# Decoding float64 weights with one 32-bit integer add on GpSimd in place of a masked two-term sum

## The chip, the cores and the metric

The kernel runs on one core of a Trainium2 chip. The metric is the device time of one execution in microseconds (us). Five engines work side by side: TensorE (PE in the profile, its weight loads PEld), VectorE (DVE), ScalarE (ACT), GpSimd (POOL) and SyncE (SP), which issues all DMAs of this kernel.

## The reference

Three layers over 2304 tokens: attention that keeps the 32 largest scores of each row, a first MLP with `g = h * cos(h)`, and a mixture of eight experts whose gate is normalised eight times over rows and columns.

```python
scores = scale * np.matmul(q, k.transpose(0, 1, 3, 2))      # (4, 8, 576, 576)
kth = np.partition(scores, -32, axis=-1)[..., -32:-31]
scores = np.where(scores >= kth, scores, -1e9)
...
h = x @ w_in;  g = h * np.cos(h);  x = g @ w_out            # w_in 512x2048, w_out 2048x512
...
for e in range(8):
    out += P[:, e:e + 1] * (np.maximum(x @ w1[e], 0.0) @ w2[e])
```

The weights `w_in` and `w_out` come as float64. The chip's engines compute in float32, so the kernel turns each float64 number, two 32-bit words, into one float32 first.

## The kernel before

The first MLP's weights are decoded in 32 blocks of 128x512 numbers, 16 of `w_in` and 16 of `w_out`. For each block `decode` loads both words of every number (`d_raw`, 512 KB), and then makes nine compute instructions: three on ScalarE that read the words (lines 349 and 351) or finish the sign (350), one Abs on ScalarE (352), two on VectorE (348 shifts and flips a bit of the high word into `d_mag`; 354 masks the sign and the exponent out), and three on GpSimd (353 multiplies the magnitude by the sign, 355 multiplies the low word's part by the signed power of two, 356 adds the two). The result lies in `win_s` or `wout_s` in SBUF and is also written to DRAM (`win_d`, `wout_d`) for later use. `d_raw` and `d_mag` are rings of four buffers; the sign takes one of the five `raw` buffers.

The program starts with three tiles of 128 tokens ("first attention" and "first mlp"): 3 tiles x 8 heads = 24 attention tiles, each with a chain of top-32 steps on VectorE (lines 480, 483, 484), softmax on ScalarE (486, 487) and GpSimd (485, 489, 491), transposes and products on TensorE (472, 496, 553). Between them stand the decode blocks. When tile 0 has its attention and all of `win_s`, its first product (650), gate (613 to 620), transposes (660) and second product (672) follow; that needs all of `wout_s`. Only when the three tiles are through the first MLP (`x2fh` and `x2fl` complete) can TensorE begin the expert products of these tokens ("fill", lines 396 to 398), which have no other input but weights and fill every gap of TensorE from then on while the attention of the other tokens runs on VectorE.

The order is not written by hand. `Plan` takes every operation with an estimated cost, its readers and writers, and a priority by engine and class (`PRIORITY`), and walks a list schedule: each engine takes the ready operation of the best priority. The costs in the `put` calls are the planner's own. In the class "decode" come the blocks; on VectorE their priority stands between the first MLP and the first attention, on GpSimd behind both. Where TensorE would stand idle in the opening, the plan inserts small matmuls that compute nothing needed (line 1088, on `ident` and `ones`).

Of the kernel before, what the change touches and what calls it, by code (L numbers as in the profile page):

```python
# [12 lines left out]
I32 = mybir.dt.int32  # L13
U32 = mybir.dt.uint32
AF = mybir.ActivationFunctionType
ALU = mybir.AluOpType
# [6 lines left out]
HALF_PI = 1.5707963267948966  # L23
# [48 lines left out]
class Plan:  # L72
# [15 lines left out]
    def buf(self, pool, shape, dtype, name):  # L88
        return Buf(self, pool, shape, dtype, name)
# [18 lines left out]
    def add(self, eng, cost, emit, reads=(), writes=(), prio=0.0, func=None, nbytes=0):  # L108
        op = Op()
        op.eng, op.cost, op.emit, op.func, op.bytes = eng, cost, emit, func, nbytes  # L110
        k = len(self.ops)
        op.prio = (prio, k)
        deps = set()

        def norm(acc):
            for a in acc:
                if isinstance(a, tuple) and isinstance(a[0], View):
                    b, lo, _ = a[0].span
                    yield b, lo + a[1], lo + a[2]
                elif isinstance(a, View):  # L120
                    yield a.span
                elif isinstance(a, Buf):
                    yield a, 0, 1 << 30
                else:
                    yield a

        pools = set()
        for b, lo, hi in norm(reads):
            pools.add(b.pool)
            for l, h, i, wr in b.log:  # L130
                if wr and l < hi and lo < h:
                    deps.add(i)
        for b, lo, hi in norm(writes):
            pools.add(b.pool)
            for l, h, i, wr in b.log:
                if l < hi and lo < h:
                    deps.add(i)
        for b, lo, hi in norm(writes):
            b.log = [e for e in b.log if not (lo <= e[0] and e[1] <= hi)]
            b.log.append((lo, hi, k, True))  # L140
        for b, lo, hi in norm(reads):
            b.log.append((lo, hi, k, False))
        for p in pools:
            for old in self.pools[p].get("after", ()):
                deps.update(self.users.get(old, ()))
                self.users[p + "<"] = True
        for p in pools:
            self.users.setdefault(p, []).append(k)
        deps.discard(k)
        op.deps = deps  # L150
        self.ops.append(op)
        return k
# [95 lines left out]
def fused_kernel(tc, kq, vv, w_in, w_out, w_gate, w1, w2, out, B=4):  # L248
# [4 lines left out]
    V, A_, G_, T_ = nc.vector, nc.scalar, nc.gpsimd, nc.tensor  # L253
# [27 lines left out]
    def put(eng, cost, emit, reads=(), writes=(), func=None, nbytes=0):  # L281
        return add(eng, cost, emit, reads, writes, PRIORITY[eng][CLASSES.index(work)], func, nbytes)

    def dma(dst, src, nbytes, reads=(), writes=(), slow=False):
        put("SP", 650.0 if slow else 475.0, lambda: nc.sync.dma_start(dst(), src()), reads, writes, nbytes=nbytes)
# [5 lines left out]
    cols = buf("cst", [128, 4], F32, "cols")  # L291
# [3 lines left out]
    put("POOL", 500, lambda: make_identity(nc, ident.ap), writes=[ident])  # L295
    put("DVE", 70, lambda: V.memset(ones.ap, 1.0), writes=[ones])
    put("DVE", 70, lambda: V.memset(zero.ap, 0.0), writes=[zero])
    for i, c in enumerate((HALF_PI, 768.0, -768.0)):
        put("DVE", 60, lambda i=i, c=c: V.memset(cols.ap[:, i : i + 1], c), writes=[(cols, i, i + 1)])
    x_d = buf("dram", [128, 4, NT], F32, "x_d")  # L300
    lg_d = buf("dram", [16, NT], F32, "lg_d")
# [35 lines left out]
    def decode(src, keep, part, low):  # L337

        raw, mag, sgn = d_raw(), d_mag(), raw_r()
        lb, lv = low
        dma(lambda: raw.ap, lambda: src.bitcast(I32), 1 << 19, writes=[raw])
        hi = lambda dt: raw.ap.bitcast(dt).rearrange("p (n t) -> p n t", t=2)[:, :, 1]
        lo = lambda: raw.ap.bitcast(U32).rearrange("p (n t) -> p n t", t=2)[:, :, 0]
        magf = lambda: mag.ap.bitcast(F32)
        put("DVE", 335, lambda: V.tensor_scalar(mag.ap, hi(I32), 3, 0x40000000, op0=ALU.logical_shift_left, op1=ALU.bitwise_xor), [raw], [mag])
        put("ACT", 613, lambda: A_.activation(sgn.ap, hi(F32), AF.Identity, bias=cols.ap[:, 1:2]), [raw, cols], [sgn])
        put("ACT", 613, lambda: A_.activation(sgn.ap, sgn.ap, AF.Sign, bias=cols.ap[:, 2:3]), [sgn, cols], [sgn])  # L350
        put("ACT", 520, lambda: A_.activation(lv(), lo(), AF.Copy, scale=2.0**-52), [raw], [lb])
        put("ACT", 520, lambda: A_.activation(magf(), magf(), AF.Abs), [mag], [mag])
        put("POOL", 1225, lambda: G_.tensor_tensor(magf(), magf(), sgn.ap, op=ALU.mult), [mag, sgn], [mag])
        put("DVE", 335, lambda: V.tensor_scalar(sgn.ap.bitcast(I32), mag.ap, -8388608, None, op0=ALU.bitwise_and), [mag], [sgn])
        put("POOL", 1225, lambda: G_.tensor_tensor(lv(), lv(), sgn.ap, op=ALU.mult), [lb, sgn], [lb])
        put("POOL", 1225, lambda: G_.tensor_tensor(lv(), magf(), lv(), op=ALU.add), [mag, lb], [lb])
        dma(keep, lv, 1 << 18, [lb], [part])

    def fresh(src, keep, part, low):
        if wide:  # L360
            decode(src, keep, part, low)
        else:
            dma(low[1], lambda: src, 1 << 18, writes=[low[0]])
            dma(keep, low[1], 1 << 18, [low[0]], [part])
# [762 lines left out]
```

## Time and profile before

| what | value |
|---|---|
| time, median of 3 runs (lowest to highest) | 2396.32 us (2395.92 to 2397.65) |
| profiled execution's own time | 2397.71 us |
| its span | 2395.9 us |
| TensorE busy | 2337.6 us (98%) |
| VectorE busy | 1844.4 us (77%) |
| ScalarE busy | 1368.1 us (57%) |
| GpSimd busy | 1287.4 us (54%) |

The page also cuts the span into 40 slices of 60 us and gives each engine's busy share in tenths. In the trace, a stretch of the span can be asked for busy time by engine, for groups of instructions by line and tile with their mean duration, and for what ended an engine's idle time.

### The profile page before, as it was taken

How to read it: one execution, taken by the hardware profiler on the slowest of the kernel's cores; microseconds unless marked ns; L12 is line 12 of the kernel's file. 1: busy time of each engine (PE TensorE's matmuls, PEld its weight loads, DVE VectorE, ACT ScalarE, POOL GpSimd, SP SyncE). 2: the span in 40 equal slices, each digit the busy share in tenths (PEclk: the TensorE clock that was granted, in tenths of full speed). 3: DMA queues.
4: the chain of work that ended last, by engine and by line, in shares of the span. 5: the costliest groups of instructions: out<-in, count | busy, mean ns of one | idle time of the engine just before them, and what ended most of it. 6: DMA issues, size and time to landing. Idle time of an engine off the chain costs nothing.

```text
span 2395.9 us, 34290 instructions
## 1 busy us (share of the span) xinstructions
PE 2337.6 (98%) x11439; PEld 1931.1 (81%) x11439; DVE 1844.4 (77%) x3371; ACT 1368.1 (57%) x2752; POOL 1287.4 (54%) x1352
## 2 busy tenths in 40 slices
PE   7889899999989999999999999999999999999999
PEld 5545699989867888888888898888888888888887
DVE  6986999999989999995166887876666666666665
ACT  7887888888878777775366776222322232222221
POOL 6986687888887666664411046433333344444440
PEclk9999999999999999999999999999999999999999
DMA  7642355554532344333343333122222221111101
GB/s 216 199 127 93 110 162 149 165 177 143 160 91 85 99 122 124 122 93 111 115 140 107 103 115 91 49 75 75 75 75 75 79 67 41 39 36 36 36 23 49
DMA packets 152465, 242.29 MB, mean 101 GB/s; under 512 B 14624, under 2 KB 61808, under 8 KB 152288
## 3 DMA queue, kind: packets, MB, share of 16 engines
q1 hardware_dynamic: 152288, 240.10, 33.4%
q8 instruction: 90, 1.47, 0.3%
q14 instruction: 87, 0.71, 0.1%
HBM read 208.18 MB, written 31.87 MB: 100 GB/s over the span
## 4 chain that ended last, share of the span: by engine, by line
PE 78%; DVE 9%; POOL 6%; ACT 3%; issue 2%; DMA 1%; SPq 0%; POOLq 0%; ACTq 0%; DVEq 0%
PE y L396 11%; PE y L398 11%; PE y L397 11%; PE g L398 3%; PE g L396 3%; PE g L397 3%; PE t L496 3%; PE h L398 2%; PE h L396 2%; PE h L397 2%; DVE wk L483 2%; DVE m L484 2%; PE t L522 1%; PE y L411 1%; PE y L408 1%
## 5 line engine op out<-in xcount | busy, mean ns | idle before, releaser
L371 POOL TENSOR_TENSOR wlo<-raw,whi 128x512 fp32r<-128x512 f32 x336 | 447.9, 1337 | 145.0 <-ACT whi L369 110.9
L484 DVE MAX8 m<-wk 128x8 f32<-128x576 f32 x432 | 318.4, 749 | 3.6
L971 DVE SCALAR_TENSOR_TENSOR acc<-y,P,acc 128x512 f32<-128x512 f32 x308 | 228.5, 747 | 98.0 <-PE y L398 97.4
L369 ACT ACTIVATE whi<-raw 128x512 fp32r<-128x512 f32 x416 | 258.5, 627 | 70.1 <-PE y L398 26.9
L483 DVE MATCH_REPLACE8 wk<-m,wk 128x576 f32<-128x576 f32 x288 | 213.9, 743 | 1.4
L396 PE MATMUL y<-whi,gh 128*128 128x512 f32 x448 | 181.7, 406 | 0.0
L398 PE MATMUL y<-whi,gl 128*128 128x512 f32 x448 | 176.2, 393 | 0.0
L396 PE MATMUL y<-gh,xh 128*128 128x512 f32 x450 | 176.0, 391 | 0.2
L397 PE MATMUL y<-wlo,gh 128*128 128x512 f32 x448 | 175.6, 392 | 0.0
L398 PE MATMUL y<-gh,xl 128*128 128x512 f32 x450 | 175.1, 389 | 0.0
L397 PE MATMUL y<-gl,xh 128*128 128x512 f32 x450 | 175.1, 389 | 0.0
L496 PE MATMUL t<-ident,ex 128*128 128x128 f32 (+1 forms) x720 | 129.0, 277 | 25.5 <-POOL ex L491 14.3
L496 PEld LDWEIGHTS t<-ident,ex 128*128 128x128 f32 (+1 forms) x720 | 84.4, 135 | 69.4 <-POOL ex L491 19.3
L478 ACT ACTIVATE sc<-s 128x288 f32<-128x288 f32 x288 | 116.6, 405 | 28.4 <-PE s L469 17.0
L486 ACT ACTIVATE ex<-sc,m 128x576 f32<-128x576 f32 x144 | 111.1, 771 | 33.0 <-DVE m L484 32.6
L491 POOL TENSOR_SCALAR ex<-ex,m 128x576 f32<-128x576 f32 x144 | 110.2, 765 | 36.2 <-DVE m L490 28.8
L514 ACT ACTIVATE ath<-t 64x128 fp32r<-64x128 f32 (+3 forms) x272 | 104.3, 395 | 32.1 <-PE t L496 31.3
L480 DVE MAX8 m<-sc 128x8 f32<-128x576 f32 x144 | 107.4, 746 | 18.6 <-ACT sc L478 18.5
L487 ACT ACTIVATE ex<-ex,m 128x576 f32<-128x576 f32 x144 | 111.3, 773 | 6.2 <-POOL m L485 1.9
L483 DVE MATCH_REPLACE8 wk<-m,sc 128x576 f32<-128x576 f32 x144 | 106.8, 742 | 0.3
L396 PEld LDWEIGHTS y<-gh,xh 128*128 128x128 f32 x450 | 84.5, 188 | 19.0 <-DVE acc L967 0.7
L398 PEld LDWEIGHTS y<-whi,gl 128*128 128x128 f32 x448 | 84.1, 188 | 19.1 <-DVE gl L777 0.2
(381 smaller groups left out, 7153.6 us busy)
## 6 DMA issues: line engine op xcount, KB each, us to landing
raw<-in_w_dram SPq DMA_DIRECT2D x384, 256.0 KB, 2.7
kq<-in_kq_dram SPq DMA_DIRECT2D x40, 576.0 KB, 3.9
raw<-win_d SPq DMA_DIRECT2D x64, 256.0 KB, 3.0
raw<-wout_d SPq DMA_DIRECT2D x64, 256.0 KB, 2.7
y_d<-st SPq DMA_DIRECT2D x56, 256.0 KB, 3.1
raw<-y_d SPq DMA_DIRECT2D x56, 256.0 KB, 2.7
d_raw<-in_w_in_dram SPq DMA_DIRECT2D x16, 512.0 KB, 4.7
d_raw<-in_w_out_dram SPq DMA_DIRECT2D x16, 512.0 KB, 3.8
```

The source lines that it names most:

```text
L369: put("ACT", act_ns(n), lambda: A_.activation(hv(), rv(), AF.Copy), [rb], [hb])
L371: put(e, c, lambda: f.tensor_tensor(lv(), rv(), hv().bitcast(F32), op=ALU.subtract), [rb, hb], [lb])
L396: T_.matmul(o(), ah(), bh(), start=start, stop=False)
L397: T_.matmul(o(), ah(), bl(), start=False, stop=False)
L398: T_.matmul(o(), al(), bh(), start=False, stop=stop)
L478: put("ACT", act_ns(288, psum=True), lambda c=c: A_.activation(sc.ap[:, c], o(), AF.Copy), [ps_s], [(sc, c.start, c.stop)])
L483: put("DVE", 669, lambda r=r, src=src: V.match_replace(wk.ap, mc(8 * r, 8), src.ap, LOWEST), [src, (m, 8 * r, 8 * r + 8)], [wk])
L484: put("DVE", 669, lambda r=r: V.max(mc(8 * r + 8, 8), wk.ap), [wk], [(m, 8 * r + 8, 8 * r + 16)])
L486: put("ACT", act_ns(S, ap=True), lambda: A_.activation(ex.ap, sc.ap, AF.Prelu, scale=-1.0, bias=mc(31), alpha=TINY), [sc, (m, 24, 32)], [ex])
L487: put("ACT", act_ns(S, ap=True) + 93.0, lambda: A_.activation(ex.ap, ex.ap, AF.Exp, scale=-0.125 / TINY, bias=mc(32), accum_out=mc(33)), [ ...
L496: T_.transpose(pt()[:p, c - c0, :], ex.ap[:, c * 128 : c * 128 + p], ident.ap)
L971: put("DVE", 663, lambda y=y, av=av, pcol=pcol: V.scalar_tensor_tensor(av(), y.ap, pcol(), av(), op0=ALU.mult, op1=ALU.add), [y, P, a], [a])
```

## The change

The three low bits of the float32 fraction, which lie in the low word, were added as a second float after masking. Now ScalarE makes of the low word the float `2 + low * 2^-51`; its bit pattern is that of 2.0 plus the low word's leading bits, rounded, at the right place of the fraction. GpSimd adds this pattern to the shifted high word as 32-bit integers. The pattern of 2.0 sets the exponent's bias by the same add, and its carry clears the top bit, so the flip of a bit on line 348, the Abs (352) and the mask (354) are gone. A multiplication by the sign follows. A block now takes three instructions on ScalarE, one on VectorE and two on GpSimd. One constant column (2.0) is set at the start.

```diff
-    for i, c in enumerate((HALF_PI, 768.0, -768.0)):
+    for i, c in enumerate((HALF_PI, 768.0, -768.0, 2.0)):
...
-        put("DVE", 335, lambda: V.tensor_scalar(mag.ap, hi(I32), 3, 0x40000000, op0=ALU.logical_shift_left, op1=ALU.bitwise_xor), [raw], [mag])
+        put("DVE", 335, lambda: V.tensor_scalar(mag.ap, hi(I32), 3, None, op0=ALU.logical_shift_left), [raw], [mag])
+        put("ACT", 613, lambda: A_.activation(lv(), lo(), AF.Identity, bias=cols.ap[:, 3:4], scale=2.0**-51), [raw, cols], [lb])
...
-        put("ACT", 520, lambda: A_.activation(lv(), lo(), AF.Copy, scale=2.0**-52), [raw], [lb])
-        put("ACT", 520, lambda: A_.activation(magf(), magf(), AF.Abs), [mag], [mag])
-        put("POOL", 1225, lambda: G_.tensor_tensor(magf(), magf(), sgn.ap, op=ALU.mult), [mag, sgn], [mag])
-        put("DVE", 335, lambda: V.tensor_scalar(sgn.ap.bitcast(I32), mag.ap, -8388608, None, op0=ALU.bitwise_and), [mag], [sgn])
-        put("POOL", 1225, lambda: G_.tensor_tensor(lv(), lv(), sgn.ap, op=ALU.mult), [lb, sgn], [lb])
-        put("POOL", 1225, lambda: G_.tensor_tensor(lv(), magf(), lv(), op=ALU.add), [mag, lb], [lb])
+        put("POOL", 1225, lambda: G_.tensor_tensor(mag.ap, mag.ap, lv().bitcast(I32), op=ALU.add), [mag, lb], [mag])
+        put("POOL", 1225, lambda: G_.tensor_tensor(lv(), magf(), sgn.ap, op=ALU.mult), [mag, sgn], [lb])
```

Lines behind `decode` move up by three, so that the softmax scaling on GpSimd, 491 before, is 488 now, and TensorE's 396 is 393. Within `decode` the numbers mean other operations: 352 is now the integer add and 353 the multiplication by the sign. Since the plan is computed, the order of everything behind changes too.

On GpSimd the decode of the first blocks stands so before; `raw` is the sign, `m` and `ex` belong to a softmax.

```order
9 L353 TENSOR_TENSOR d_mag_144<-d_mag_144,raw_146 128x512
10 L355 TENSOR_TENSOR win_s<-win_s,raw_146 128x512
11 L485 TENSOR_SCALAR m_81<-m_81 128x1
12 L356 TENSOR_TENSOR win_s<-d_mag_144,win_s 128x512
13 L353 TENSOR_TENSOR d_mag_158<-d_mag_158,raw_161 128x512
14 L489 TENSOR_SCALAR m_81<-m_81 128x1
15 L355 TENSOR_TENSOR win_s<-win_s,raw_161 128x512
16 L491 TENSOR_SCALAR ex_178<-ex_178,m_81 128x576
17 L356 TENSOR_TENSOR win_s<-d_mag_158,win_s 128x512
```

And so now, from the same place.

```order
9 L352 TENSOR_TENSOR d_mag_145<-d_mag_145,win_s 128x512
10 L353 TENSOR_TENSOR win_s<-d_mag_145,raw_152 128x512
11 L352 TENSOR_TENSOR d_mag_159<-d_mag_159,win_s 128x512
12 L352 TENSOR_TENSOR d_mag_170<-d_mag_170,win_s 128x512
13 L482 TENSOR_SCALAR m_81<-m_81 128x1
14 L353 TENSOR_TENSOR win_s<-d_mag_159,raw_168 128x512
15 L353 TENSOR_TENSOR win_s<-d_mag_170,raw_181 128x512
16 L352 TENSOR_TENSOR d_mag_179<-d_mag_179,win_s 128x512
17 L486 TENSOR_SCALAR m_81<-m_81 128x1
```

Three blocks end before the first softmax's second small step (486), where one ended before the same step (489). Over the whole decode, its last instruction on GpSimd stood behind 21 of the 24 softmax scalings (491) and three gates (613, 614), at row 174; it stands behind 20 of them (488) and two gates now, at row 136.

On VectorE the same stretch before, with the shift (348), the mask (354) and the top-32 steps between them.

```order
11 L348 TENSOR_SCALAR d_mag_165<-d_raw_122 128x512
12 L483 MATCH_REPLACE wk_140<-m_81,wk_140 128x576
13 L354 TENSOR_SCALAR raw_146<-d_mag_144 128x512
14 L484 MAX m_81<-wk_140 128x8
15 L348 TENSOR_SCALAR d_mag_176<-d_raw_124 128x512
```

And now; 480 is the MATCH_REPLACE and 481 the MAX.

```order
12 L348 TENSOR_SCALAR d_mag_170<-d_raw_123 128x512
13 L480 MATCH_REPLACE wk_141<-m_81,wk_141 128x576
14 L348 TENSOR_SCALAR d_mag_179<-d_raw_125 128x512
15 L481 MAX m_81<-wk_141 128x8
```

The 32 masks are gone from this engine; no instruction waits there for GpSimd's first product any more.

On TensorE, the fill begins behind the last logits of the three tiles (628). Before, attention of other tokens (468, 469, 496) is mixed in at once.

```order
346 L628 MATMUL y_380<-x2fl,wg 8x128
347 L396 MATMUL g<-x2fh,whi_1939 128x384
348 L397 MATMUL g<-x2fl,whi_1939 128x384
349 L398 MATMUL g<-x2fh,wlo_1950 128x384
350 L468 MATMUL s<-kh_1568,qt_1562 128x288
351 L469 MATMUL s<-kl_1575,qt_1562 128x288
```

Now the fill stands alone there for a while.

```order
332 L625 MATMUL y_331<-x2fl,wg 8x128
333 L393 MATMUL g<-x2fh,whi_1773 128x384
334 L394 MATMUL g<-x2fl,whi_1773 128x384
335 L395 MATMUL g<-x2fh,wlo_1785 128x384
336 L393 MATMUL g<-x2fh,whi_1773 128x384
```

Ahead of the first fill matmul stand 22 score products of the later attention (468) before and 18 now. Of the matmuls on `ident` and `ones` (1088) the plan has 139 before and 111 now. ScalarE has 32 instructions of decode less, and four more table loads: one pair (sine of the gates, exponential of the softmax) ahead of the first fill, and one pair among the gates of the next 512 tokens.

## Rows read from the trace of the kernel before

**Rows 1.** The page's 40 slices: busy share in tenths, each 60 us.
```profile
PE   7889899999989999999999999999999999999999
DVE  6986999999989999995166887876666666666665
POOL 6986687888887666664411046433333344444440
```
**Rows 2.** Stretches: length, busy us (instructions) by engine, TensorE's granted clock, DMA share, GB/s.
```profile
13.00:202.00 189.00, 166.21 (x770) 100.94 (x769) 169.19 (x323) 160.40 (x321) 163.48 (x167) 0.94 0.56 175
202.00:280.00 78.00, 71.87 (x315) 39.95 (x313) 59.03 (x118) 61.12 (x128) 41.01 (x60) 1.00 0.21 67
280.00:660.00 380.00, 376.84 (x2205) 340.65 (x2205) 371.15 (x838) 318.46 (x746) 313.97 (x383) 1.00 0.53 160
660.00:760.00 100.00, 87.61 (x405) 69.90 (x403) 85.29 (x130) 80.67 (x138) 78.04 (x69) 0.98 0.28 85
760.00:1080.00 320.00, 319.33 (x1672) 265.09 (x1671) 315.36 (x695) 246.22 (x559) 207.30 (x270) 1.00 0.38 112
1080.00:2396.00 1316.00, 1307.86 (x6066) 1110.19 (x6064) 842.53 (x1264) 498.70 (x862) 482.93 (x402) 1.00 0.24 73
```
**Rows 3.** The same view for line 1088 alone (PE, PEld), and its sum over 0 to 280.
```profile
13.00:202.00 189.00, 41.71 (x264) 36.43 (x264) 0.94 0.56 175
sum 280.00, PE 46.09 PEld 39.53; mean PE 15.36 PEld 13.18
```
**Rows 4.** The chain that ended last, 13 to 202 us, shares by line.
```profile
by line: DVE wk L483 11.2%; DVE m L484 8.1%; issue 7.5%; DVE d_mag L348 6.8%; PE t L553 5.8%; POOL win_s L355 5.6%; POOL d_mag L353 4.8%; POOL win_s L356 4.6%; DVE raw L354 4.6%; DMA d_raw<-in_w_in_dram 4.5%; PE s L472 4.3%; POOL wout_s L35
```
**Rows 5.** Groups by line, 13 to 202 us, GpSimd's: busy us, mean ns | idle before.
```profile
L353 POOL TENSOR_TENSOR d_mag<-d_mag,raw 128x512 f32<-128x512 f32 x32 | 42.0, 1317 | 15.0 <-ACT d_mag L352 14.5
L356 POOL TENSOR_TENSOR wout_s<-d_mag,wout_s 128x512 f32<-128x512 f32 x16 | 23.9, 1492 | 0.6
L355 POOL TENSOR_TENSOR wout_s<-wout_s,raw 128x512 f32<-128x512 f32 x16 | 20.7, 1297 | 3.2 <-DVE raw L354 2.5 <-DVE m L490 0.4
L355 POOL TENSOR_TENSOR win_s<-win_s,raw 128x512 f32<-128x512 f32 x16 | 20.7, 1297 | 3.2 <-DVE raw L354 2.7 <-DVE m L490 0.4
L356 POOL TENSOR_TENSOR win_s<-d_mag,win_s 128x512 f32<-128x512 f32 x16 | 20.5, 1285 | 0.2
L491 POOL TENSOR_SCALAR ex<-ex,m 128x576 f32<-128x576 f32 x21 | 16.7, 797 | 6.2 <-DVE m L490 5.6 <-PE s L472 0.5
```
**Rows 6.** The page's group of the weights' subtraction on GpSimd, over the whole span.
```profile
L371 POOL TENSOR_TENSOR wlo<-raw,whi 128x512 fp32r<-128x512 f32 x336 | 447.9, 1337 | 145.0 <-ACT whi L369 110.9
```
**Rows 7.** One line's instructions: ns min/median/max, first and last start.
```profile
L348 DVE TENSOR_SCALAR d_mag<-d_raw x32: 401/866/1492, 13.2 to 178.5; 128x512 int32<-128x512 int32 x32
L356 POOL TENSOR_TENSOR wout_s<-d_mag,wout_s x16: 1261/1279/2312, 103.5 to 200.5; 128x512 f32<-128x512 f32 x16
```
**Rows 8.** Groups by line, 13 to 202 us, VectorE's.
```profile
L484 DVE MAX8 m<-wk 128x8 f32<-128x576 f32 x68 | 50.2, 748 | 0.5
L348 DVE TENSOR_SCALAR d_mag<-d_raw 128x512 int32<-128x512 int32 x32 | 27.4, 858 | 11.3 <-POOL win_s L356 6.1 <-POOL wout_s L356 3.7 <-DMA d_raw<-in_w_in_dram 1.5
L354 DVE TENSOR_SCALAR raw<-d_mag 128x512 int32<-128x512 int32 x32 | 20.8, 651 | 1.7 <-POOL d_mag L353 1.7
```
**Rows 9.** Groups by line, 13 to 202 us, ScalarE's.
```profile
L349 ACT ACTIVATE raw<-d_raw,cols 128x512 f32<-128x512 f32 x32 | 24.3, 760 | 1.3 <-DMA d_raw<-in_w_in_dram 1.3
L352 ACT ACTIVATE d_mag<-d_mag 128x512 f32<-128x512 f32 x32 | 19.9, 621 | 3.5 <-DVE d_mag L348 3.5
L351 ACT ACTIVATE win_s<-d_raw 128x512 f32<-128x512 uint32 x16 | 10.6, 661 | 0.0
L617 ACT ACT_TABLE_LOAD x3 | 3.8, 1283 | 0.1
```
**Rows 10.** First fill matmuls of line 396, 0 to 330 us; columns as in rows 7.
```profile
L396 PE MATMUL g<-x2fh,whi x17: 331/338/522, 279.4 to 329.8; 128*128 128x384 f32 x17
```

## The prediction

> **What bounds the kernel now.** I read the page's slices first [rows 1]: from the sixth slice on TensorE stands at 9 in every slice but one, and ahead of that at 7 to 9 while VectorE and GpSimd stand at 6 to 9. Then the stretches [rows 2]. From 280 to 660 us, from 760 to 1080 and from 1080 to the end TensorE is busy for all but 3.2, 0.7 and 8.1 us, so there the time is TensorE's own work, and VectorE, though at 98% until 1080, keeps nobody waiting. Between 660 and 760 it idles for 12.4 us. The opening is the other exception: 22.8 us idle from 13 to 202 and 6.1 from 202 to 280, and 46.1 us of its busy time are the needless matmuls of line 1088 [rows 3], 41.7 of them in the decode's stretch. So some 75 us of slack lie in the opening, and since TensorE's real work is the same before and after, whatever shortens the opening shortens the kernel, as long as no later stretch gives it back. 75 us is the most that any change to the opening could bring.
>
> What makes the opening long is to be seen in the decode's stretch, 13 to 202 us: VectorE is busy for 169.2 us of 189 (0.895), GpSimd for 163.5 (0.865), ScalarE for 160.4 (0.849) [rows 2]. No one of them is full, and all three are near it: each waits in turn for the others. The chain of that stretch says which instructions stand in it [rows 4]: the top-32 steps with 19.3%, and then decode: line 348 with 6.8%, 355 on `win_s` 5.6%, 353 4.8%, 356 on `win_s` 4.6%, 354 4.6%, together 26.4% or 50 us, with the parts on `wout_s` still to come where the row is cut. So decode is on the path, not beside it.
>
> **The change, engine by engine.** All in the stretch from 13 to 202 us.
>
> GpSimd: three instructions a block become two. The five groups of decode sum to 127.8 us for 96 instructions [rows 5], 1.33 us each; 32 fewer are 42.6 us, and 163.5 becomes 120.9. This takes the integer add at the price of a float instruction, and the trace shows no integer add on GpSimd. Its nearest rows: multiplication (353, 355), addition (356) and, far from decode, subtraction (371) have means of 1285 to 1492 ns [rows 5, 6], so the price of two tensor inputs here doesn't ask which operation it is; I take 1.33. The bounds: below, the one-input 128x576 group of line 491 with 0.80 us [rows 5]; above, the slowest instruction of line 356 with 2.31 us [rows 7]. With 0.80 GpSimd has 104 us, with 2.31 152 us: below today's 163.5 either way. The Trainium skill, page "GPSIMD Engine Reference", section "Engine selection", says that an add whose inputs and output are all one 32-bit integer type is exact and that the cores add integers natively; it gives no duration, and no run here shows one yet.
>
> VectorE: the mask (354) goes, 20.8 us [rows 8]. Line 348 loses its second operation; its shortest instance has 401 ns and the mean 858 [rows 7, 8], while the top-32 step of 484 stands at 748 with no spread of that kind. So 32 x 0.457 = 14.6 us of line 348 are stretch that comes and goes. The shift itself I leave at 401 ns, since it still passes the same 512 elements; between nothing and all of the stretch is open. GpSimd's busy share falls from 0.865 to about 0.73 (120.9 of some 165), which takes 15% or 2.2 us off the stretch. 169.2 becomes 146.2. The Trainium skill, page "SBUF — State Buffer", section "Who interferes with whom", has a reason for the stretch: a scalar operation of VectorE in its two-port mode and a GpSimd instruction take a shared pair of ports in turn, each for the whole instruction. By that rule line 348 keeps meeting GpSimd, only more rarely, and the sum stays; were the stretch of another origin and gone altogether, VectorE would have 133.8 us and the stretch 150 us at today's share.
>
> ScalarE: the Abs (352) goes, 19.9 us. The Copy of the low word (351, 661 ns) becomes an Identity with a bias column; line 349 is one already, on the same kind of input, with 760 ns [rows 9]: 32 x 0.099 = 3.2 us more. 160.4 becomes 143.7. The extra memset of a column is one instruction among the first, while all wait for the first loads: nothing, and its length if that cover were gone.
>
> The sum: if VectorE stays as tightly packed as today, the stretch lasts 146.2 / 0.895 = 163 us, 26 less than 189. By ScalarE it lasts 143.7 / 0.849 = 169, 20 less. GpSimd would need 120.9 / 0.865 = 140 and no longer counts. I take the middle of the first two, 23 less. Upwards of that speak VectorE's waits for GpSimd's decode, 6.1 + 3.7 + 1.7 = 11.5 of its 20 us idle [rows 8]: they stand for the end of a chain of six steps on three engines (348, 352 to 356) that now has three, and if all of them vanish the stretch is 146.2 + 8.3 = 154.5 us, 34 less. Downwards speaks the integer add at 2.31: 152 / 0.865 = 176 us, 13 less.
>
> What is late next: the top-32 steps of the 24 attention tiles on VectorE, which the change doesn't touch, and ScalarE beside them. From 202 to 280 us little changes in kind. The order puts one softmax and one gate more behind the last decode instruction, work that is counted in the sum already, and one pair of table loads more ahead of the fill at 1.28 us each [rows 9]. ScalarE has 61 us of 78 there [rows 2], so of these 2.6 us I put 1 on the path. Fewer products of the later attention (18 instead of 22) stand ahead of the first fill matmul; they are moved and not saved. Together 22 less. The profiled execution has 2397.7 us, 1.8 above its span and 1.4 above the median of 2396.3; 2397.7 - 22 = 2375.7, and against the median 2374.
>
> **The rivals.** First, a slower integer add, the case that ends slower than before. GpSimd's load is then 163.5 - 127.8 + 32 x (1.33 + p) = 78.3 + 32p us for a price of p. It passes today's 163.5 at p = 2.66 us, twice a float instruction, and from there GpSimd holds the opening; at four times the float price, 5.3, it is 248 us, the stretch 248 / 0.865 = 287 and the kernel 2396 + 98 = 2494. For it: the operation and its type are nowhere in the trace. Against it: three operations at one price [rows 5, 6].
>
> Second, the gain is given back between 660 and 760 us. There the fill of the first three tiles is used up, and TensorE lives on the first MLP of the next 512 tokens, whose gates pass through VectorE, ScalarE and GpSimd, busy for 85, 81 and 78 us of the 100 [rows 2]. TensorE reaches this place earlier, and by the order with less of the attention behind it; four score products of 22 are two attention tiles, fourteen top-32 steps of 0.75 us or 10 us [rows 8]. If VectorE is what it waits for, its idle time grows from 12.4 us by up to the whole 22, and the pair of table loads there adds 2.6: between 2384 and 2399. For it: that stretch is the one later place where other engines end TensorE's waits. Against it: VectorE has 23 us less to do by then too, so that it comes as much earlier as TensorE.
>
> Third, more than 34 us: the whole stretch of line 348 goes, and with it the waits; 133.8 + 8.3 = 142 us on VectorE, 47 less, but ScalarE at 143.7 would have to be full. Between 2350 and 2362.
>
> **How the numbers follow.** The forecast, 9 to 34 us less: 0.76, with 2374. The slower add: 0.07. The gain given back: 0.12, half of it within 0.2% (4.8 us, about what a measurement of this kernel can tell from no change). More than 34: 0.05. The range of 2362 to 2388 holds the forecast with the integer add's upper bound and leaves out the slower add, the half of the second rival that ends at no change, and the third, 0.18 in all. Faster by over 0.2%: 0.76 + 0.06 + 0.05 = 0.87; within: 0.06; slower: 0.07.
>
> **What would show it.** The integer add's group on GpSimd near 1.3 us; GpSimd's decode near 85 us in 64 instructions; line 348 still spread between 0.40 and 1.5 us; the last decode instruction to start near 177 us instead of 200.5 [rows 7] and the first fill matmul near 258 instead of 279 [rows 10]; line 1088 and TensorE's idle time together 20 or more us lower up to there; and the stretch without fill some 20 us earlier with about 12 us idle. The forecast is wrong if the integer add is over 2.3 us, if ScalarE fills up first and the opening shrinks by less than 13 us, or if TensorE idles some 30 us around 640 to 740.

## The result and the profile after

| what | before | after |
|---|---|---|
| time, median (lowest to highest), 4 runs each | 2396.76 us (2395.92 to 2397.65) | 2369.63 us (2367.24 to 2372.10) |
| profiled execution: time, span | 2397.71, 2395.9 us | 2372.10, 2370.0 us |
| last decode instruction on GpSimd starts | 200.5 us | 165.1 us |
| first fill matmul on TensorE starts | 279.4 us | 254.6 us |
| span behind the first fill matmul | 2116.5 us | 2115.4 us |

The ratio of after to before is 0.9887 (95% interval 0.9870 to 0.9904): 27 us less, between 23 and 31. In the profiled executions the spans differ by 25.9 us, and 24.8 us of that are gone when the fill begins.

The page's slices after, busy share in tenths, each 59 us; they answer to [rows 1].

```profile
PE   7999999999989999999999999999999999999999
DVE  6995999999989999994177786876666666666665
POOL 6754878887886666664501036433333344444440
```

TensorE is at 9 from the second slice on, apart from one around 680 us; GpSimd has become lighter in the first slices. The stretches after, with the columns of [rows 2] (length, busy us of TensorE, its weight loads, VectorE, ScalarE, GpSimd, granted clock, DMA share, GB/s):

```profile
13.00:169.00 156.00, 143.18 (x652) 85.49 (x651) 136.67 (x274) 139.40 (x276) 114.23 (x132) 0.96 0.66 209
169.00:202.00 33.00, 32.85 (x151) 17.87 (x151) 18.06 (x35) 23.88 (x43) 8.72 (x13) 1.00 0.10 31
280.00:660.00 380.00, 376.90 (x2167) 336.12 (x2165) 369.11 (x822) 318.90 (x724) 313.52 (x375) 1.00 0.51 154
660.00:760.00 100.00, 89.29 (x424) 71.23 (x425) 88.17 (x147) 79.86 (x147) 76.34 (x69) 0.98 0.33 93
760.00:1080.00 320.00, 320.00 (x1685) 267.15 (x1684) 315.22 (x695) 246.35 (x558) 207.14 (x270) 1.00 0.37 112
0.00:280.00 280.00, 257.55 (x1177) 159.50 (x1178) 221.69 (x454) 227.89 (x464) 178.23 (x221) 0.97 0.52 161
```

The last of these stretches in the kernel before, and then the needless matmuls alone after the change (line 1085 now; TensorE and its weight loads):

```profile
0.00:280.00 280.00, 245.99 (x1099) 145.31 (x1099) 230.07 (x449) 224.04 (x452) 205.20 (x232) 0.96 0.48 147
0.00:280.00 280.00, 38.84 (x222) 32.68 (x222) 0.97 0.52 161
```

The last decode instructions and the first fill matmuls after, with the columns of [rows 7] and [rows 10]:

```profile
L353 POOL TENSOR_TENSOR wout_s<-d_mag,raw x16: 1267/1275/1452, 75.6 to 165.1; 128x512 f32<-128x512 f32 x16
L393 PE MATMUL g<-x2fh,whi x28: 331/337/423, 254.6 to 323.3; 128*128 128x384 f32 x28
```

Decode is over at 166 us instead of 202. Until then ScalarE is now the busiest of the three at 139.4 us of 156 (0.89), VectorE has 136.7 (0.88) and GpSimd 114.2 (0.73). Behind 280 us nothing has changed that a reader could point to: TensorE idles for 10.7 us between 660 and 760 where it idled for 12.4.

The groups of decode from 13 to 202 us on GpSimd, busy us, mean ns | idle before; they answer to [rows 5]:

```profile
L352 POOL TENSOR_TENSOR d_mag<-d_mag,wout_s 128x512 int32<-128x512 int32 x16 | 21.6, 1352 | 1.7 <-ACT wout_s L349 1.5
L352 POOL TENSOR_TENSOR d_mag<-d_mag,win_s 128x512 int32<-128x512 int32 x16 | 20.9, 1311 | 13.4 <-ACT win_s L349 13.1
L353 POOL TENSOR_TENSOR wout_s<-d_mag,raw 128x512 f32<-128x512 f32 x16 | 20.6, 1290 | 5.8 <-ACT raw L351 5.6
L353 POOL TENSOR_TENSOR win_s<-d_mag,raw 128x512 f32<-128x512 f32 x16 | 20.3, 1274 | 4.0 <-ACT raw L351 3.7 <-DVE d_mag L348 0.3
```

The first two rows are the integer add. It costs what the float instructions beside it cost: 1311 and 1352 ns against 1274 and 1290. Decode takes 83.4 us of GpSimd instead of 127.8.

The shift on VectorE from 13 to 280 us and the low word's Identity on ScalarE from 13 to 169 us, in the same columns; they answer to [rows 8] and [rows 9]:

```profile
L348 DVE TENSOR_SCALAR d_mag<-d_raw 128x512 int32<-128x512 int32 x32 | 22.2, 694 | 10.5 <-POOL win_s L353 5.3 <-DMA d_raw<-in_w_out_dram 2.1 <-DMA d_raw<-in_w_in_dram 2.0
L349 ACT ACTIVATE win_s<-d_raw,cols 128x512 f32<-128x512 uint32 x16 | 12.1, 758 | 0.8 <-DMA d_raw<-in_w_in_dram 0.8
```

The shift's mean fell from 858 to 694 ns. Single instances show where the rest of its stretch comes from (start, length in us):

```profile
69.55 0.41 DVE L348 TENSOR_SCALAR d_mag<-d_raw 128x512 int32<-128x512 int32 x1
72.41 1.27 POOL L352 TENSOR_TENSOR d_mag<-d_mag,wout_s 128x512 int32<-128x512 int32 x1
72.55 1.41 DVE L348 TENSOR_SCALAR d_mag<-d_raw 128x512 int32<-128x512 int32 x1 [1.01 <-POOL m L482]
```

The first meets no GpSimd instruction and takes 0.41 us. The second begins while the integer add runs and ends 0.28 us behind it. So it is throughout: 13 of the 32 instances take 0.40 to 0.43 us, and each of the other 19 ends 0.28 to 0.29 us behind a GpSimd instruction that was running when it began. In the kernel before, 19 of the 32 do the same.

The chain that ended last, 13 to 202 us after the change, answers to [rows 4]:

```profile
by line: PE t L550 13.7%; PE y L669 11.8%; PE s L469 7.8%; DVE wk L480 6.4%; DVE m L481 6.0%; DMA d_raw<-in_w_out_dram 5.8%; PE h L647 5.8%; PE y L647 5.6%; PE t L493 4.8%; DVE d_mag L348 4.5%; DMA d_raw<-in_w_in_dram 3.1%; ACT ex L484 2.6%
```

No GpSimd instruction of decode is among its first entries any more. TensorE's own products of the first attention (550, 469) and the first MLP (647, 669) lead it, with 44.7% together. Part of that is the 36 us behind the end of decode, which this window now holds; from 13 to 169 us alone the four lines have 37.7%, and the top-32 steps (480, 481) 15.1% instead of 12.4%.

### The profile page after: what moved, and what is told of

Same layout as the page of the kernel before. It is cut to its first block, busy times and chain, and to the rows that moved or that the text cites. A ratio compares the mean times of both kernels' runs of the same rounds, so it can differ in the third digit from the quotient of the medians.

```text
span 2370.0 us, 34117 instructions
## 1 busy us (share of the span) xinstructions
PE 2326.2 (98%) x11383; PEld 1923.5 (81%) x11383; DVE 1817.3 (77%) x3340; ACT 1357.3 (57%) x2724; POOL 1243.0 (52%) x1320
## 4 chain that ended last, share of the span: by engine, by line
PE 84%; DVE 6%; POOL 4%; ACT 3%; DMA 2%; issue 1%; SPq 0%; POOLq 0%; DVEq 0%; ACTq 0%
PE y L393 12%; PE y L395 12%; PE y L394 12%; PE g L393 4%; PE g L395 4%; PE g L394 4%; PE t L493 3%; PE h L393 3%; PE h L395 3%; PE h L394 3%; PE t L519 1%; PE s L465 1%; PE y L404 1%; PE y L405 1%; PE y L408 1%
## 5 line engine op out<-in xcount | busy, mean ns | idle before, releaser
L395 PE MATMUL y<-gh,gl 128*128 128x512 f32 x254 | 99.5, 392 | 0.0
```

The costliest lines, as they stand in the source:

```text
L395: T_.matmul(o(), al(), bh(), start=False, stop=stop)
```

## Experiments

Every kernel below is the changed kernel with one edit. Its figure is the median of 4 to 11 runs, its ratio that to the kernel before, measured beside it on the same chip (median 2395.9 to 2397.1). The load theory says: each of VectorE, ScalarE and GpSimd is nearly full in the opening, and the gain is the work that the change took from them. The rival, the chain theory: the gain is the shorter chain of dependent steps from word to float.

**All the removed work put back, with no reader.**

```diff
         dma(keep, lv, 1 << 18, [lb], [part])
+        put("POOL", 1225, lambda: G_.tensor_tensor(magf(), lv(), lv(), op=ALU.mult), [lb], [mag])
+        put("DVE", 335, lambda: V.tensor_scalar(sgn.ap.bitcast(I32), lv().bitcast(I32), -8388608, None, op0=ALU.bitwise_and), [lb], [sgn])
+        put("ACT", 520, lambda: A_.activation(magf(), lv(), AF.Abs), [lb], [mag])
```

> The changed kernel with all three added instructions per block: a multiplication on GpSimd, a mask on VectorE, an Abs on ScalarE, none of them read by anyone. Work per engine is as before the change, but a block's own chain stays at three steps. The outputs stay the reference's. Load theory: 2392 to 2400 us, the whole gain gone. Chain theory: 2370 to 2380 us.

Measured: 2395.08 us, ratio 0.9996 (0.9987 to 1.0004). The whole gain is gone although a block's chain still has three steps. The first fill matmul (columns of [rows 10]):

```profile
L396 PE MATMUL g<-x2fh,whi x16: 332/337/657, 282.1 to 319.6; 128*128 128x384 f32 x16
```

At 282.1 us it starts about where it did before (279.4). Up to there VectorE, ScalarE and GpSimd are busy for 232.3, 228.5 and 199.5 us; before the change it was 229.5, 223.6 and 204.7. The scratch writes hold the block's buffers longer, which is a second way in which this kernel resembles the one before. What shows of it is small: line 348 waits for the release of a `d_mag` buffer for 9.2 us here, for 9.8 before the change and for 5.3 after it. What the longer hold does to the order that the plan makes wasn't separated.

**One engine's work put back at a time**, with the first, second or third of those lines alone.

> The changed kernel with one more two-input GpSimd multiplication per block (32 in all), which reads the finished block and writes a scratch that nobody reads (the block's own d_mag buffer, held that much longer, as before the change). The outputs stay the reference's. Load theory: what counts in the opening is how much work each engine has, GpSimd gets its 42 us back (114 us of the 156 from 13 to 169 us becomes 156) and sets the opening at its old share of 0.865, 180 us: about 2390 us, nearly all of the gain gone. Chain theory: what counts is that a block has three dependent steps instead of six; the added step has no reader, and the time stays at 2370 to 2376 us.

Measured: 2382.38 us, ratio 0.9945 (0.9932 to 0.9957): 13 us of the gain gone. The added GpSimd instructions took 34 us, not 42; the row is shown at the end.

> The changed kernel with one more masking instruction per block on VectorE, of the shape of the one that was removed, reading the finished block and writing the sign's buffer, which nobody reads any more. The outputs stay the reference's. Load theory: VectorE gets 13 to 21 us back, 137 us of 156 becomes 150 to 158, at its share of 0.895 a stretch of 168 to 176 us: 2381 to 2390 us. Chain theory: 2368 to 2374 us.

Measured: 2377.18 us, ratio 0.9923 (0.9909 to 0.9936): 7.5 us gone, between the two expectations, and the interval leaves the changed kernel's only just. The added masks took 27.6 us, not 13 to 21, so work on VectorE cost less per us than I had reckoned.

> The changed kernel with one more Abs per block on ScalarE, reading the finished block and writing a buffer that nobody reads. The outputs stay the reference's. Load theory: ScalarE, the busiest of the three after the change with 139 us of 156, gets 20 us back, 159 us at 0.89 is 179 us: about 2392 us. Chain theory: 2368 to 2374 us.

Measured: 2385.15 us, ratio 0.9951 (0.9939 to 0.9963): 15.5 us gone. The first fill matmuls of the three, in that order:

```profile
L394 PE MATMUL g<-x2fh,whi x24: 332/336/426, 263.3 to 321.8; 128*128 128x384 f32 x24
L394 PE MATMUL g<-x2fh,whi x28: 331/337/423, 256.8 to 330.0; 128*128 128x384 f32 x28
L394 PE MATMUL g<-x2fh,whi x22: 333/337/426, 270.0 to 329.6; 128*128 128x384 f32 x22
```

Spans of 2378.0, 2374.9 and 2385.9 us less these starts give 2114.7, 2118.1 and 2115.9 us. So in these three the time is set, to within some 3 us, where the fill starts, as before and after the change (2116.5 and 2115.4). Each engine alone brings back a part: 13, 7.5 and 15.5 us, 36 in sum against 25 for all three together. I expected of ScalarE and GpSimd alone that nearly all would go (2392 and 2390 us), which holds for neither: the work counts on each engine, but one engine's load put back alone doesn't hold the opening as all three together do.

**A long chain without the work.**

```diff
         put("POOL", 1225, lambda: G_.tensor_tensor(mag.ap, mag.ap, lv().bitcast(I32), op=ALU.add), [mag, lb], [mag])
+        put("DVE", 80, lambda: V.tensor_scalar(mag.ap[:, 0:1], mag.ap[:, 0:1], -1, None, op0=ALU.bitwise_and), [mag], [mag])
+        put("ACT", 200, lambda: A_.activation(magf()[:, 0:1], magf()[:, 0:1], AF.Copy), [mag], [mag])
+        put("DVE", 80, lambda: V.tensor_scalar(mag.ap[:, 0:1], mag.ap[:, 0:1], -1, None, op0=ALU.bitwise_and), [mag], [mag])
```

> The changed kernel with three tiny steps of one column (128x1) between the integer add and the multiplication by the sign, VectorE, ScalarE, VectorE, which change nothing: a block's chain has six dependent steps over three engines again, as before the change, with nearly none of the work (some 0.3 to 0.4 us a block on ScalarE and VectorE each). The outputs stay the reference's. Load theory: 2370 to 2377 us, and the part over 2370 is the small steps' own length, 10 us on two engines at most. Chain theory: 2382 to 2396 us.

Measured: 2372.11 us, ratio 0.9903 (0.9888 to 0.9918), 2.5 us over the changed kernel and within its interval. The steps in the trace, 13 to 280 us:

```profile
L354 ACT ACTIVATE d_mag<-d_mag 128x1 f32<-128x1 f32 x32 | 6.3, 197 | 3.2 <-DVE d_mag L353 2.8
L355 DVE TENSOR_SCALAR d_mag<-d_mag 128x1 int32<-128x1 int32 x32 | 4.5, 140 | 2.3 <-ACT d_mag L354 2.3
L353 DVE TENSOR_SCALAR d_mag<-d_mag 128x1 int32<-128x1 int32 x32 | 4.4, 139 | 1.9 <-POOL d_mag L352 1.9
```

Six dependent steps over three engines cost next to nothing, as long as they are short. With the kernel that has all the work and a chain of three steps, this decides against the chain theory, which counts steps. That leaves the load theory, with one thing not separated from it: how long a block holds its buffers, which the added work lengthens and these short steps hardly do.

**The same instructions in another order.**

```diff
-        put("DVE", 335, lambda: V.tensor_scalar(mag.ap, hi(I32), 3, None, op0=ALU.logical_shift_left), [raw], [mag])
+        put("DVE", 600, lambda: V.tensor_scalar(mag.ap, hi(I32), 3, None, op0=ALU.logical_shift_left), [raw], [mag])
...
-        put("POOL", 1225, lambda: G_.tensor_tensor(lv(), magf(), sgn.ap, op=ALU.mult), [mag, sgn], [lb])
+        put("POOL", 1290, lambda: G_.tensor_tensor(lv(), magf(), sgn.ap, op=ALU.mult), [mag, sgn], [lb])
```

> The changed kernel with other costs for decode in the planner alone (VectorE 600, ScalarE 660, GpSimd 1290 ns, nearer to the trace): the same instructions in another order. The outputs stay the reference's. It shows how much of a difference of a few us is the luck of an order. Load theory: 2366 to 2374 us. Rival, that the gain lies in the particular order that the plan came to: over 2376 us.

Measured: 2369.45 us, ratio 0.9888 (0.9871 to 0.9904), the changed kernel's own time. The gain doesn't hang on the one order that the plan had come to: another gives the same.

**What decode still costs: no sign at all.** The two sign instructions on ScalarE and the multiplication are left out, and with them the `raw` buffer that held the sign.

```diff
-        put("ACT", 613, lambda: A_.activation(sgn.ap, hi(F32), AF.Identity, bias=cols.ap[:, 1:2]), [raw, cols], [sgn])
-        put("ACT", 613, lambda: A_.activation(sgn.ap, sgn.ap, AF.Sign, bias=cols.ap[:, 2:3]), [sgn, cols], [sgn])
-        put("POOL", 1225, lambda: G_.tensor_tensor(mag.ap, mag.ap, lv().bitcast(I32), op=ALU.add), [mag, lb], [mag])
-        put("POOL", 1225, lambda: G_.tensor_tensor(lv(), magf(), sgn.ap, op=ALU.mult), [mag, sgn], [lb])
+        put("POOL", 1225, lambda: G_.tensor_tensor(lv().bitcast(I32), mag.ap, lv().bitcast(I32), op=ALU.add), [mag, lb], [lb])
```

> The changed kernel without the sign: both ScalarE instructions and the GpSimd multiplication of each block are left out (48 and 41 us), so that the weights of the first MLP come out as magnitudes and the outputs aren't the reference's. Decode keeps one VectorE, one ScalarE and one GpSimd instruction a block. It shows how far the opening could still be shortened by a cheaper decode. Load theory: fill starts at 230 to 245 us, 2345 to 2360 us in all, VectorE's 137 us in the decode's stretch being the bound. Rival, that the opening is bound elsewhere by now: 2363 to 2371 us.

Measured: 2347.84 us, ratio 0.9803 (0.9789 to 0.9818), 22 us below the changed kernel, the fill starting at 227.2 us:

```profile
L390 PE MATMUL g<-x2fh,whi x36: 333/336/429, 227.2 to 323.7; 128*128 128x384 f32 x36
```

So the opening was not yet bound elsewhere.

**One of the two engines alone.** First ScalarE (the sign taken straight from the high word), then GpSimd (the multiplication left out, the sign made and not used).

```diff
-        put("ACT", 613, lambda: A_.activation(sgn.ap, hi(F32), AF.Identity, bias=cols.ap[:, 1:2]), [raw, cols], [sgn])
-        put("ACT", 613, lambda: A_.activation(sgn.ap, sgn.ap, AF.Sign, bias=cols.ap[:, 2:3]), [sgn, cols], [sgn])
+        put("ACT", 613, lambda: A_.activation(sgn.ap, hi(F32), AF.Sign), [raw], [sgn])
```

> The changed kernel with the sign taken by one ScalarE instruction (Sign straight of the high word) instead of two, which takes 32 x 0.75 = 24 us off ScalarE. What it leaves out is the flush of numbers too small for float32 to zero; the outputs for these inputs stay the reference's. So far the span stood 2113 to 2118 us behind the first fill matmul in six kernels, so it should again. Load theory: one engine's 20 us on ScalarE cost 15.5 us, taking 24 off should give back less, since VectorE (137 us of 156) stays: the fill starts at 242 to 248 instead of 255 us, 2357 to 2365 us in all. Rival, that VectorE's top-32 steps alone now bind: 2366 to 2371 us.

Measured: 2368.96 us, ratio 0.9890 (0.9876 to 0.9905). No gain in time, which lies in the rival's range. The fill started earlier all the same:

```profile
L392 PE MATMUL g<-x2fh,whi x30: 333/337/428, 248.2 to 329.7; 128*128 128x384 f32 x30
```

The opening is 6.4 us shorter in this profile, about as the load theory had it (242 to 248), and the span stood 2122.8 us behind the first fill matmul, outside the 2113 to 2118 that I had expected. Behind it TensorE idled for 23.4 us instead of 21.6, and its clock stood at 0.94 instead of 1.00 from 600 to 660 us; the rest of those 7 us stays open. So the time doesn't show that VectorE's steps alone bind the opening.

> The changed kernel without the multiplication by the sign on GpSimd (41 us there); both ScalarE instructions that make the sign stay, and nobody reads them. The first MLP's weights come out as magnitudes, so the outputs aren't the reference's. Beside the kernel without any sign (2348 us) and the one with 28 us less on ScalarE (2369 us) it separates the two engines. If GpSimd's load holds the opening through its meetings with VectorE (line 348: 694 ns in the changed kernel, 556 without any sign): 2348 to 2358 us. If both engines have to be relieved together: 2360 to 2370 us.

Measured: 2365.92 us, ratio 0.9872 (0.9855 to 0.9890), within the changed kernel's interval. The shift on VectorE in this kernel and in the one without any sign, 13 to 280 us:

```profile
L348 DVE TENSOR_SCALAR d_mag<-d_raw 128x512 int32<-128x512 int32 x31 | 18.8, 608 | 9.8 <-DMA d_raw<-in_w_out_dram 5.1 <-DMA d_raw<-in_w_in_dram 4.7
L348 DVE TENSOR_SCALAR d_mag<-d_raw 128x512 int32<-128x512 int32 x32 | 17.8, 556 | 0.8 <-DMA d_raw<-in_w_in_dram 0.8
```

The shift was nearly as short as in the kernel without any sign, and the time was not. I had put GpSimd's weight down to these meetings; that falls. The 41 us taken from GpSimd alone are worth some 4 us, inside the intervals, the first sign step taken from ScalarE alone (26 us by the two kernels' groups) no time, both engines relieved together 22. From this kernel to the one without any sign only the two ScalarE steps go, with the sign's buffer, and that is 18 of the 22 us. No run takes both steps from ScalarE and leaves GpSimd its multiplication, so whether the two engines have to be relieved together, or ScalarE of both steps, stays open.

**Work moved to VectorE.** The sign is put in by one VectorE instruction, ahead of the add; the two sign instructions on ScalarE and the multiplication go, as in the kernel without any sign. To that kernel the edit is this one line:

```diff
+        put("DVE", 660, lambda: V.scalar_tensor_tensor(mag.ap, hi(I32), -2147483648, mag.ap, op0=ALU.bitwise_and, op1=ALU.bitwise_xor), [raw, mag], [mag])
```

> The changed kernel with the sign put in by one VectorE instruction per block, which takes the high word's top bit and flips it into the shifted word ahead of the integer add, instead of two ScalarE instructions and the GpSimd multiplication. It leaves out the flush to zero of numbers too small for float32, and a zero would come out as 2.0; these inputs have neither. Work in the opening: ScalarE 48 us less, GpSimd 41 less, VectorE 32 x 0.66 to 1.3 = 21 to 42 us more. Load theory, with prices from the runs so far: without the sign altogether 2348 us, and 14 us more on VectorE cost 7.5 us before, so 21 to 42 us cost 11 to 23: 2359 to 2371 us. Rival, VectorE alone sets the opening by now: 2372 to 2390 us.

Measured: 2379.89 us, ratio 0.9926 (0.9913 to 0.9940): 10 us slower than the changed kernel, with 48 us less on ScalarE and 41 less on GpSimd. The stretches from 20 to 80 us, columns as above:

```profile
20.00:40.00 20.00, 17.04 (x63) 10.93 (x61) 19.92 (x41) 10.48 (x22) 10.02 (x14) 0.83 0.94 311
40.00:60.00 20.00, 17.77 (x78) 11.54 (x77) 20.00 (x37) 12.58 (x27) 11.76 (x13) 0.82 0.99 328
60.00:80.00 20.00, 17.43 (x92) 11.11 (x90) 19.91 (x41) 12.59 (x28) 12.41 (x14) 1.00 0.90 306
```

VectorE is busy for 59.8 us of 60, ScalarE and GpSimd for 35.6 and 34.2. The first fill matmul:

```profile
L391 PE MATMUL g<-x2fh,whi x26: 333/336/427, 257.1 to 329.4; 128*128 128x384 f32 x26
```

The comparison that comes nearest to VectorE alone is that with the kernel without any sign, which lacks this instruction and nothing else. The instruction takes 24.7 us and line 348 6.5 us more than there, 31 together; the fill starts 29.9 us later and the time is 32 us longer. Here one engine does hold the opening, and each us on it costs one. I had carried over a price per us from the run with the added mask, where VectorE had room, and with 14 us of masks instead of 27.6. The rival was right. Against the changed kernel the fill is only 2.5 us later; most of the 8.1 us between the two spans lies behind it (2121.0 us instead of 2115.4).

**More needless matmuls, to keep TensorE's clock up.** In the kernel with one sign step, the granted clock stood at 0.83, 0.82 and 0.59 from 20 to 80 us, means over its two levels of 1.2 and 2.4 GHz, so that the last stretch ran mostly at the lower one; TensorE had been busy for 17.2 and 18.5 us of the 20 ahead of it:

```profile
20.00:40.00 20.00, 17.15 (x80) 12.95 (x80) 19.76 (x37) 15.14 (x33) 16.77 (x19) 0.83 0.91 291
40.00:60.00 20.00, 18.50 (x68) 9.65 (x69) 19.08 (x34) 15.64 (x34) 17.54 (x20) 0.82 0.89 268
60.00:80.00 20.00, 20.00 (x67) 13.12 (x68) 13.97 (x32) 12.50 (x28) 11.54 (x15) 0.59 0.67 197
```

```diff
-                n = int(0.65 * gap / beat_ns)
+                n = int(0.95 * gap / beat_ns)
```

> The kernel with one sign instruction on ScalarE, with the needless matmuls of the opening planned at 0.95 of each gap instead of 0.65 (122 instead of 71), and nothing else. In its trace without them TensorE's granted clock stood at 0.83, 0.82 and 0.59 in the three stretches of 20 us from 20 to 80 us. If the 28 us that ScalarE got back there were lost to that clock: clock over 0.9 there, 2358 to 2365 us. Rival, that VectorE's steps bind and ScalarE's time was worth nothing: 2366 to 2372 us whatever the clock. It leaves out the flush of numbers too small for float32 to zero.

Measured: 2366.15 us, ratio 0.9874 (0.9861 to 0.9888), with the clock at 1.00 in all three stretches. Some 3 us less than without, inside the intervals, and the fill started at 246.5 us instead of 248.2.

> The changed kernel with the needless matmuls planned at 0.95 of each gap instead of 0.65 (185 instead of 111). The outputs stay the reference's. In the changed kernel's trace the clock stood at 0.74 and 0.92 from 20 to 60 us. If the clock there holds the opening back: 2363 to 2367 us. If not, the fuller gaps only stand in the way of the real matmuls: 2368 to 2376 us.

Measured: 2374.14 us, ratio 0.9905 (0.9892 to 0.9919), clock 1.00 from 20 to 80 us; no gain, the intervals overlap, and the fill started at 256.6 us instead of 254.6. The clock of these 60 us is not what holds the opening. No kernel that leaves nothing of the computation out beats the changed one.

## Why the prediction was right, point by point

- **Where the time is.** The opening with its slack, and nothing later: right. The span behind the first fill matmul was 2116.5 us before and 2115.4 after. In the twelve kernels above it was 2111.7 to 2122.8, while the start of the fill went from 227 to 282 us: the start of the fill decides most of the time, but differences of a few us can lie behind it.
- **GpSimd.** The integer add at 1.33 us: 1311 and 1352 ns. Decode 85 us forecast, 83.4 measured. The rival of a slow integer add is out. The Trainium skill, page "GPSIMD Engine Reference", section "Engine selection", says that the cores add integers natively; these rows fit that.
- **VectorE.** The mask gone, and line 348 at 694 ns instead of 858: 5.2 us less where I took 2.2. The stretch was mis-sized by 3 us, and the reason that I gave for its fall doesn't hold. The two engines met as often as before, in 19 of 32 blocks; what fell is the time that the GpSimd instruction still had to run when 348 began, from 0.87 to 0.60 us in the mean. Nor does the mean follow GpSimd's load: it was 675 ns with all the work put back and 856 with one sign step less on ScalarE. That the two take turns is shown by the instances above. The Trainium skill's page "SBUF — State Buffer" says in "Who interferes with whom" that of a VectorE instruction in the two-port mode and a GpSimd instruction the one that issues first gets the shared pair of ports for the whole instruction. The trace agrees: of the 0.40 us that line 348 takes alone, 0.28 still follow when the GpSimd instruction has ended.
- **ScalarE.** 758 ns for the Identity against 760 taken.
- **The packing.** I scaled each engine's load by its old share and took the middle of two answers, 23 us, less 1 for the tail. The opening became 24.8 us shorter. Up to the end of decode (13 to 166.4 us) VectorE was busy for 0.88 of the time and ScalarE for 0.90, near the shares that I had used, so the step is sound in size, and the load theory under it was borne out by the runs, as far as they separate it; what it said about one engine as the bound was not: the single loads sum to 36 us and no engine returns the whole gain alone.
- **The end of decode.** 177 us forecast, 165.1 measured; the 11 us came back behind it, where one softmax and one gate more stood, and the tail from the last decode instruction to the fill grew from 79 to 89.5 us. I had counted that work in the sum and not in the place: VectorE had 134.9 us of work up to the end of decode, not 146.2, and ScalarE 137.3, not 143.7. That the shorter decode and the longer tail offset one another to within 3 us of the forecast is in part luck.
- **The slack.** TensorE's idle time and needless matmuls up to 280 us fell from 34.0 + 46.1 to 22.4 + 38.8 us, 19 less; 20 or more was forecast. (The 75 us of slack that I had counted left out the first 13 us.) Of the other 6 us by which the opening is shorter, some 3 are the clock's, 0.97 instead of 0.96; the rest must be work that now stands behind the first fill matmul.
- **The second rival.** Nothing was given back: 660 to 760 us idled for 10.7 us instead of 12.4.
- **The next bound.** I named VectorE's top-32 steps. In the chain their share fell from 19.3% to 12.4%, and TensorE's products lead it. The run with the sign on VectorE shows that VectorE binds when it alone is full. In the changed kernel no one engine was found to bind alone: the runs took work from ScalarE and from GpSimd, none took any from VectorE.

## What to carry to other kernels

Where three engines are each near nine tenths full and wait in turn for one another, a cheaper formula pays by the work it takes from all of them; taking 26 or 41 us from one alone paid nothing or hardly anything here, and moving work onto one of them cost 10 us. Once one engine is full and the others have room, as VectorE there, each us on it was paid in full. Before costing a chain, test it: three more dependent steps of 0.14 to 0.2 us in each of 32 blocks cost 2.5 us here, within the interval. And look for the event behind which the rest of the program has a nearly fixed length, here the first fill matmul (2112 to 2123 us), and read every edit by when that event comes, and by what changed behind it. A mean that is stretched by another engine is read instance by instance: which instruction was running when it began says more than the other engine's load.

## What the runs showed of the hardware that was not expected

A GpSimd multiplication of a tile with itself is cheaper than one of two tiles: in the kernel with GpSimd's work put back, 13 to 280 us, against the product by the sign in the same kernel.

```profile
L353 POOL TENSOR_TENSOR win_s<-d_mag,raw 128x512 f32<-128x512 f32 x16 | 20.4, 1275 | 0.9 <-DVE d_mag L348 0.3
L355 POOL TENSOR_TENSOR d_mag<-win_s 128x512 f32<-128x512 f32 x16 | 17.0, 1064 | 0.2
```

The first reads two buffers, the second one buffer twice: 1275 and 1064 ns. In the kernel with all the work put back the second had means of 1103 and 1190 ns, with waits for VectorE in them; its median was 1042 ns in both kernels, against 1274 to 1278 for the first.
